# One written-out instruction order: a planner that knows the port shared by VectorE and GpSimd

## The chip, the cores and the metric

The kernel runs on one core of a Trainium2 chip. The metric is the device time of one execution in microseconds. A core has five engines with queues of their own: TensorE (PE, with its weight loads PEld), VectorE (DVE), ScalarE (ACT), GpSimd (POOL) and SyncE (SP), which issues the DMAs here. TensorE's clock has two levels, 1.2 and 2.4 GHz; the granted clock was full (1.00) in every stretch of the profile but the last microseconds.

## The reference

Attention over 4 batches, 8 heads, 768 positions and head size 64, in which a position sees itself, the 127 before it (`window` = 128) and the first four (`n_sink` = 4). Its output, as 3072 rows of 512, goes through a gated layer of 1536 units:

```
scores = q @ k.T / sqrt(64);  keep = (pos < n_sink) | (0 <= rel < window)
a = softmax(where(keep, scores, -1e9));  attn = a @ v
x = attn as [3072, 512]
out = (sigmoid(x @ w_gate) * (x @ w_val)) @ w_out
```

Inputs to the attention are float32, the three weight matrices float64. The output is float32.

## The kernel before

The kernel is one long straight program. The work is described to a planner (`Plan`), which simulates the engines on the host while the program is built, and writes all instructions out in the order that its simulation gave. The hardware then keeps that order on each engine. Every instruction recorded by the planner has line 575, so groups are told apart by tiles.

A step of work (`Plan.op`) has a priority (smaller is more urgent) and a list of ways, each with an engine and a time in ns. In `run`, each engine that is free takes its most urgent ready step for which buffers are free. The second and third way of a step wait at a priority that is worse by 1 and 2. The times come from small formulas: `vec`, `act`, `pool` and `mac`. Three more things set the order. All times on DVE, ACT and POOL are multiplied by `CROWD` = 1.1 until 350 us. Up to `HELD` = 45 us, an engine leaves a step aside when a more urgent one that only waits for steps under way becomes due within `HOLD` = 0.6 of the step's length. PE gets filler matmuls (`warm`, m<-ident) up to 130 us where too little of a period was busy.

The work itself:

- 96 attention units (`attend`, u = 0 to 95), one for each group of 256 positions and each head, with priority u. The first 20 are in plain float32. In the others each operand is split into a rounded high part and the rest (`copy` makes the high part, on ACT or else DVE; `rest` the difference, on POOL or else DVE). A unit does its scores on PE (tiles a), mask and row minimum on DVE, exp on ACT, the sum's reciprocal, a scaling of P, a transpose on PE, a split of the transposed P (wt) with two selections on POOL, the product with v on PE, and two additions on DVE (low, xf).
- 36 decodings of the float64 weights (`decode`, tiles wst to ws), each a load, a scaling on ACT, a byte step (ACT, or DVE, or POOL) and two integer steps on DVE. Their priorities are `DS1 + DR1 * n` = 8 + 0.3 n, on the attention units' scale. After the last of them (`DECODED`) the tiles lo may be loaded.
- The weights are then split too (`halves`, priority from 16 on; `thirds`, sums for the paired feed, from 250 us on, priority from 25 on); the low parts go to DRAM and come back as tiles lo, chunk by chunk.
- The feed (`feed`): nine chunks of rows, in plain float32 for the first, then single or double groups (`feed_plain`), and three chunks with two groups at once (`feed_pair`, seven products instead of eight). Each has 12 passes over f: products into m on PE, tanh on ACT, DVE steps into th and cv, a split into gh and gl, and the last products into o or a. Its steps on DVE and ACT come before all others (priority from -1000 on), on PE after the attention (10000 on).

Of the kernel before, what the change touches and what calls it, by code (L numbers as in the profile page):

```python
# [28 lines left out]
FLOOR = 0.75  # L29
CROWD = 1.1  # L30
HOLD = 0.6
HELD = 45000.0
GAP = 1.5
# [10 lines left out]
DS1 = 8.0  # L44
DR1 = 0.3
DS2 = 18.0
# [5 lines left out]
ALT = 1  # L52
# [240 lines left out]


class Op:
    def __init__(self, prio, ways, dma, busy):
# [5 lines left out]
class Plan:  # L302
# [37 lines left out]
    def run(self, warm, fill_ns, fill):  # L340
# [13 lines left out]
        def put(o):  # L354
            for i, (e, _, _) in enumerate(o.ways):
                heapq.heappush(waiting[e], ((o.prio + i * ALT, o.seq), o))

# [8 lines left out]
        dma_free, window, active, cold = 0.0, 1, [0.0] * 1000, True  # L366
        HAM = 4096 / 1.2

        def busy(a, b, frac):
# [6 lines left out]
        while events:  # L376
# [25 lines left out]
            for e in free:  # L402
# [4 lines left out]
                while waiting[e] or unsure:  # L407
# [25 lines left out]
                    if first != e and BACK:  # L433
# [5 lines left out]
                        if wait < BACK:  # L439
                            held.append((key, o))  # L440
                            continue
                    ns, fn = next((ns, fn) for w, ns, fn in o.ways if w == e)
                    if e in soon and now < HELD:
                        soon[e] = [x for x in soon[e] if x.due > now and id(x) not in done]
                        if any(
                            x.prio + GAP < o.prio and x.due < now + HOLD * ns for x in soon[e]
                        ):
                            held.append((key, o))
                            continue
# [4 lines left out]
                    if e in "VAG" and now < CROWDED:  # L454
                        ns *= CROWD
                    if e == "PE":
                        while window * HAM <= now:
                            x = active[window - 1] / HAM
                            cold = x < HOT if cold else x < WARMED
                            window += 1  # L460
                        if cold:
                            ns *= 2
                        busy(now, now + ns, o.busy)
# [44 lines left out]
def kernel(  # L508
# [71 lines left out]

    def vec(cols, fast=False):
        return 80 + (0.95 if fast else 1.25) * cols

# [3 lines left out]
    def pool(cols):  # L587
        return 250 + 2.2 * cols

# [5 lines left out]

    def copy(prio, cols, out, in_, r, w, psum=False, start=0.0):

        plan.op(
            prio,
            [  # L600
                ("A", act(cols, psum), lambda: A.copy(out=out(), in_=in_())),
                ("V", vec(cols, not psum), lambda: V.tensor_copy(out=out(), in_=in_())),
            ],
            r, w, start=start,
        )

    def rest(prio, cols, out, in0, in1, r, w, psum=False):

        plan.op(
            prio,  # L610
            [
                (
                    "G", pool(cols), lambda: G.tensor_tensor(
                        out=out(), in0=in0(), in1=in1().bitcast(F32), op=ALU.subtract
                    ),
                ),
                (
                    "V", vec(cols), lambda: V.tensor_tensor(
                        out=out(), in0=in0(), in1=in1().bitcast(F32), op=ALU.subtract
                    ),  # L620
                ),
            ][1 if psum else 0 :],
            r, w,
        )

    def f32(ap):
        return ap if ap.dtype == F32 else ap.bitcast(F32)
# [212 lines left out]
    def attend(u, b, h, t0, T, XR):  # L840
# [44 lines left out]
        for t in range(T):  # L885
# [28 lines left out]
            def exp(t=t):  # L914
# [6 lines left out]
            plan.op(  # L921
                u, [("V", 290 if first else 600, top)],
                [sc, (MASKS, 3), (MASKS, min(t0 + t, 2))], [sc, (P, t)],
# [21 lines left out]
        def mul():  # L945
            for t in range(T):
# [6 lines left out]
                )),  # L953
                ("G", 300, guard(G)), ("V", 300, guard(V)),
            ], [], [rs]
# [3 lines left out]
        )  # L959
        plan.op(u, [("G", 760, share), ("A", 720, mul), ("V", 720, scale)], [rs], [P])  # L960

        if not plain:
# [21 lines left out]
            plan.op(  # L984
                u, [("G", pool(W), spread(G)), ("V", vec(W), spread(V))], [turned, OWN], [sk]
            )
# [7 lines left out]
        def turn():  # L994
# [4 lines left out]
            if plain:  # L999
# [3 lines left out]
                )  # L1003

        def split():
            f = 1 - prev
            if T > f:
                G.affine_select(
                    out=w()[:, :, f:T, 0], in_=f32(w())[:, :, f:T, 1],
                    pattern=[[0, Z], [0, T - f], [-1, 128]], compare_op=ALU.is_gt, fill=0.0,  # L1010
                    base=0, channel_multiplier=1,
                )
            G.affine_select(
                out=w()[:, :, :, 1], in_=f32(w())[:, :, :, 1],
                pattern=[[0, Z], [0, T], [1, 128]], compare_op=ALU.is_ge, fill=0.0, base=0,
                channel_multiplier=-1,
            )
# [5 lines left out]
        if not plain:  # L1023
# [6 lines left out]
            )  # L1030
        plan.op(u, [("G", 980.0 if plain else 1370.0, split)], [], [wt])

        o = 64 * y
        if plain:
            vhl, sk = vraw, SK0[h // 2 % 2]
            copy(
                u, 128, lambda: sk()[o : o + T * NS], lambda: tp()[0 : T * NS, W : W + 128], [tp],
                [(sk, y)], True,
            )
        else:  # L1040
            vhl = tile([128, L, 2 * D], F32R, "vhl", BUFS["vhl"])
            copy(u, L * D, lambda: vhl()[:, :, 0:D], vraw, [vraw], [(vhl, 0)])
            rest(
                u, L * D, lambda: vhl()[:, :, D : 2 * D], vraw, lambda: vhl()[:, :, 0:D],
                [vraw, (vhl, 0)], [(vhl, 1)],
            )
# [118 lines left out]
    def minus(p, cols, out, a, b, r, w, add=False, start=0.0):  # L1165
        plan.op(
            p, [
                (
                    n, ns, lambda E=E: E.tensor_tensor(
                        out=out(), in0=a(), in1=b(), op=ALU.add if add else ALU.subtract  # L1170
                    ),
                ) for n, ns, E in (("G", pool(cols), G), ("V", vec(cols), V))
            ], r, w, start=start,
        )
# [26 lines left out]
    def decode(prio, src, whole):  # L1201
# [19 lines left out]
                )),  # L1221
                ("V", 900.0, lambda: V.tensor_scalar(
                    out=by(2), in0=by(1), scalar1=13, scalar2=None, op0=ALU.logical_shift_right
                )),
                ("G", 1300.0, lambda: G.tensor_scalar(
                    out=by(2), in0=by(1), scalar1=2.0**-13, scalar2=-8191.0 / 16384, op0=ALU.mult,
# [5 lines left out]
        plan.op(  # L1232
            prio, [("V", vec(512, True), lambda: V.tensor_scalar(
                out=ai(), in0=ai(), scalar1=3, scalar2=None, op0=ALU.logical_shift_left
# [3 lines left out]
        plan.op(  # L1238
            prio, [("V", vec(512), lambda: V.scalar_tensor_tensor(
                out=ai(), in0=hw(), scalar=-2147483641, in1=ai(), op0=ALU.bitwise_and,  # L1240
# [243 lines left out]
    def feed_pair(ci, tcs, f, O):  # L1484
# [22 lines left out]
        def turn(i, src, r):  # L1507
# [42 lines left out]
        plan.op(  # L1550
            pr, [("V", vec(512), lambda: V.scalar_tensor_tensor(
                out=th(), in0=th(), scalar=1.0, in1=cv(), op0=ALU.add, op1=ALU.mult
# [102 lines left out]
```

## Time and profile before

| | |
|---|---|
| median of 3 runs | 808.45 us (807.86 to 809.13) |
| profiled execution | 808.95 us, span 807.2 us |
| PE busy | 767.6 us, 95% |
| DVE busy | 636.8 us, 79% |
| POOL busy | 508.3 us, 63% |
| ACT busy | 440.6 us, 55% |
| DMA | 185.59 MB, mean 230 GB/s |

Busy time is the time in which an engine's instructions are recorded as running, waits for a port included. PE's ends are modelled, so that a very short gap between matmuls is not seen. A stretch's length less PE's busy time in it is PE's idle time there.

### The profile page before, as it was taken

The page shows a single profiled execution, that of the slowest core. Times are in us where ns is not written, and L with a number is a line of the kernel's source. Part 1 is how long each engine was busy: PE and PEld are TensorE (multiplying, and loading weights), DVE is VectorE, ACT ScalarE, POOL GpSimd, SP SyncE. Part 2 cuts the span into 40 slices and gives each one's busy share as a digit, 9 for nine tenths or more (in the row PEclk, how much of TensorE's full clock was granted, in tenths as well). Part 3 has the DMA queues.
Part 4 walks back from the last instruction along what each step waited for, and adds up shares of the span by engine and source line. Part 5 has one row for each costly group of instructions (what it writes and reads, how often), then busy time and mean ns, then how long its engine had stood idle before and what let it go on. Part 6 is the DMA issues. An engine that isn't in the chain of part 4 may idle for free. (4 is left out here: it accounts for less than half of the span.)

```text
span 807.2 us, 16573 instructions
## 1 busy us (share of the span) xinstructions
PE 767.6 (95%) x5084; PEld 686.2 (85%) x5084; DVE 636.8 (79%) x1806; ACT 440.6 (55%) x1258; POOL 508.3 (63%) x675
## 2 busy tenths in 40 slices
PE   7999988999999999999999998999999999999996
PEld 6876766799999888799889887899898899999995
DVE  5899889855999999968999999989999994444111
ACT  7788877624777655446776544467656651111200
POOL 4678788745688889646887776757777862111111
PEclk9999999999999999999999999999999999999998
DMA  6999985996777899886677666677776666666761
GB/s 157 231 272 283 302 249 180 340 293 204 223 235 240 258 335 307 289 272 203 203 239 238 217 204 193 201 249 248 223 223 204 188 218 187 208 193 215 226 188 57
DMA packets 137264, 185.59 MB, mean 230 GB/s; under 512 B 49360, under 2 KB 61648, under 8 KB 137168
## 3 DMA queue, kind: packets, MB, share of 16 engines
q1 hardware_dynamic: 137168, 184.45, 73.8%
q8 instruction: 43, 0.70, 0.3%
q14 instruction: 53, 0.43, 0.2%
HBM read 159.24 MB, written 25.17 MB: 228 GB/s over the span
## 5 line engine op out<-in xcount | busy, mean ns | idle before, releaser
L575 PE MATMUL m<-ws,ws 128*128 128x256 f32 x1680 | 316.1, 285 | 4.3 <-DVE th L575 2.9
L575 PE MATMUL m<-ws,lo 128*128 128x256 f32 x1272 | 293.1, 282 | 1.3 <-POOL ws L575 0.7
L575 PEld LDWEIGHTS m<-ws,ws 128*128 128x128 f32 x1680 | 265.6, 189 | 16.1 <-DVE th L575 4.2
L575 PEld LDWEIGHTS m<-ws,lo 128*128 128x128 f32 x1272 | 212.4, 189 | 2.2 <-DMA lo<-wlo_d 1.0
L575 POOL TENSOR_SCALAR_AFFINE_SELECT wt<-wt 128x512 fp32r<-128x512 f32 (+3 forms) x192 | 125.2, 652 | 41.0 <-DVE wt L575 20.7
L575 POOL TENSOR_TENSOR gl<-th,gh 128x256 fp32r<-128x256 f32 (+1 forms) x53 | 53.4, 1008 | 123.7 <-DVE gh L575 89.4
L575 ACT ACTIVATE th<-m 128x256 f32<-128x256 f32 x108 | 41.5, 384 | 127.7 <-PE m L575 78.9
L575 ACT ACTIVATE P<-P,negm_all 128x144 f32<-128x144 f32 x192 | 78.8, 411 | 38.1 <-DVE negm_all L575 36.1
L575 DVE SCALAR_TENSOR_TENSOR th<-th,m 128x256 f32<-128x256 f32 x72 | 29.8, 414 | 64.3 <-PE m L575 63.2
L575 PE MATMUL o<-ws,gh 128*128 128x512 f32 x192 | 77.2, 402 | 1.3 <-DVE total L1606 0.8
L575 PE MATMUL o<-ws,gl 128*128 128x512 f32 x192 | 75.9, 395 | 1.1 <-DVE gl L575 0.7
L575 PE MATMUL o<-lo,gh 128*128 128x512 f32 x192 | 75.1, 391 | 0.0
L575 DVE CUSTOM_DVE_ANT_0 P<-a,am 128x144 f32<-128x144 f32 x192 | 58.5, 305 | 10.2 <-PE a L575 4.0
L575 POOL TENSOR_TENSOR ws<-ws,ws 128x512 fp32r<-128x512 f32 (+1 forms) x47 | 60.7, 1298 | 6.9 <-ACT ws L575 2.6
L575 PE MATMUL a<-wt,vhl 128*128 128x256 f32 (+2 forms) x282 | 61.2, 327 | 3.2 <-POOL wt L575 2.3
L575 POOL TENSOR_TENSOR hi<-qkT,hi 64x256 fp32r<-64x256 f32 x60 | 49.9, 832 | 15.7 <-issue 5.6
L575 PEld LDWEIGHTS a<-wt,vhl 128*128 128x128 f32 x282 | 47.1, 189 | 13.3 <-POOL wt L575 4.8
L575 ACT CAST hi<-qkT 128x656 fp32r<-128x656 f32 (+1 forms) x70 | 49.2, 704 | 10.5 <-PE a L575 6.7
L575 PE MATMUL a<-ident,P 128*128 128x128 f32 (+1 forms) x212 | 40.4, 277 | 9.9 <-POOL P L575 3.3
L575 DVE TENSOR_TENSOR cv<-m,cv 128x256 f32<-128x256 f32 x72 | 30.0, 417 | 24.8 <-ACT cv L575 14.7
L575 PE MATMUL a<-hi 128*128 128x272 f32 (+1 forms) x152 | 44.8, 305 | 3.0 <-DVE negm_all L575 1.1
L575 POOL TENSOR_TENSOR kl<-qkT,hi 128x400 fp32r<-128x400 f32 (+1 forms) x43 | 45.3, 1053 | 1.6
(144 smaller groups left out, 1723.5 us busy)
## 6 DMA issues: line engine op xcount, KB each, us to landing
lo<-wlo_d SPq DMA_DIRECT2D x396, 256.0 KB, 3.4
wlo_d<-ws SPq DMA_DIRECT2D x72, 256.0 KB, 4.4
qkT<-in_qk_dram SPq DMA_DIRECT2D x52, 328.0 KB, 3.9
qkT<-in_qk_dram SPq DMA_DIRECT2D x24, 264.0 KB, 3.8
wst<-in_moe_w_gate_dram SPq DMA_DIRECT2D x12, 512.0 KB, 5.4
wst<-in_moe_w_val_dram SPq DMA_DIRECT2D x12, 512.0 KB, 5.2
wst<-in_moe_w_out_dram SPq DMA_DIRECT2D x12, 512.0 KB, 4.8
out_dram<-w SPq DMA_DIRECT2D x24, 256.0 KB, 3.7
```

Source lines behind the costliest of these rows:

```text
L575: return lambda *a, **kw: tc.keep_in_program_order(op(*a, **kw))
```

## The change

Some costs get a mark, `Port`: steps on DVE that read two SBUF operands or copy and scale within SBUF, and all large steps on POOL. The planner holds one time, `port`, up to which the port is taken. A marked step is lengthened by its wait for the port, less `LEAD` = 130 ns, and then takes the port. On DVE a marked step is left aside until the port is within 230 ns of free. A marked way of a step whose first way is ACT is left aside while ACT has under `BACKA` = 500 ns ahead of it. `CROWD` becomes 1.0 (no stretching), `HELD` 800 us (the holding rule is on throughout), `DR1` 0.2 (decodings at 8 + 0.2 n). The third way of a step now waits like the second. Costs are set anew, and the two selections on POOL are two steps of the plan. The core of the diff:

```diff
-CROWD = 1.1
+CROWD = 1.0
+LEAD = 130.0
+PWAIT = 100.0
+BACKA = 500.0
+ALTR = 1.0
-HELD = 45000.0
+HELD = 800000.0
-DR1 = 0.3
+DR1 = 0.2
+class Port(float):
+    pass
...
-                heapq.heappush(waiting[e], ((o.prio + i * ALT, o.seq), o))
+                alt = ALT if o.ways[0][0] == "A" else ALTR
+                heapq.heappush(waiting[e], ((o.prio + min(i, 1) * alt, o.seq), o))
...
+                    through = isinstance(ns, Port)
+                    if through and first == "A" and BACKA:
+                        mine = (o.prio, o.seq)
+                        wait = max(free[first] - now, 0.0) + sum(
+                            x.ways[0][1] for k, x in waiting[first]
+                            if k < mine and id(x) not in done and x.ways[0][0] == first
+                        )
+                        if wait < BACKA:
+                            held.append((key, o))
+                            continue
+                    if through and e == "V" and port - LEAD - PWAIT > now:
+                        held.append((key, o))
+                        n += 1
+                        heapq.heappush(events, (port - LEAD - PWAIT, n, None))
+                        continue
...
+                    if through:
+                        ns += max(0.0, port - now - LEAD)
+                        port = now + ns + (70.0 if e == "V" else 0.0)
...
-    def vec(cols, fast=False):
-        return 80 + (0.95 if fast else 1.25) * cols
+    def vec(cols):
+        return 80 + 1.0 * cols
+    def one(cols):
+        return Port(75 + 0.52 * cols)
+    def two(cols):
+        return Port(60 + 1.07 * cols)
     def pool(cols):
-        return 250 + 2.2 * cols
+        return Port(170 + 2.17 * cols)
...
-                ("V", vec(cols, not psum), lambda: V.tensor_copy(out=out(), in_=in_())),
+                ("V", vec(cols) if psum or apart else one(cols), lambda: V.tensor_copy(out=out(), in_=in_())),
...
-                ("V", 900.0, lambda: V.tensor_scalar(
+                ("V", Port(900.0), lambda: V.tensor_scalar(
-                ("G", 1300.0, lambda: G.tensor_scalar(
+                ("G", Port(1340.0), lambda: G.tensor_scalar(
...
-        plan.op(u, [("G", 980.0 if plain else 1370.0, split)], [], [wt])
+        plan.op(u, [("G", Port(180 + 0.9 * Z * (T - f) * 128), split)], [], [wt])
+        plan.op(u, [("G", Port(180 + 0.9 * Z * T * 128), rest_of)], [], [wt])
```

## Rows read from the trace of the kernel before

**Rows 1.** Page, part 1: busy us (share of the span) xinstructions.

```profile
PE 767.6 (95%) x5084; PEld 686.2 (85%) x5084; DVE 636.8 (79%) x1806; ACT 440.6 (55%) x1258; POOL 508.3 (63%) x675
```

**Rows 2.** Stretches: length, busy of PE, PEld, DVE, ACT, POOL, clock, DMA, GB/s.

```profile
40.00:120.00 80.00, 74.43 (x348) 55.58 (x347) 71.97 (x170) 63.73 (x139) 63.54 (x71) 1.00 0.90 277
...
120.00:160.00 40.00, 34.84 (x202) 27.80 (x201) 35.05 (x97) 29.77 (x72) 32.54 (x41) 1.00 0.79 257
...
160.00:280.00 120.00, 119.57 (x859) 112.35 (x859) 96.69 (x310) 69.59 (x222) 83.55 (x127) 1.00 0.79 243
...
280.00:340.00 60.00, 55.31 (x367) 48.56 (x366) 59.52 (x131) 32.48 (x93) 50.00 (x57) 1.00 0.93 310
...
380.00:520.00 140.00, 132.29 (x915) 120.71 (x914) 133.40 (x389) 84.57 (x261) 104.46 (x139) 1.00 0.69 214
...
520.00:660.00 140.00, 138.46 (x956) 126.17 (x956) 132.35 (x378) 86.71 (x262) 104.27 (x134) 1.00 0.72 221
...
660.00:800.00 140.00, 139.04 (x963) 129.11 (x962) 48.52 (x117) 21.98 (x61) 26.56 (x31) 1.00 0.61 189
```

**Rows 3.** Timeline: start, us, instruction; one step in two consecutive passes.

```profile
697.71 0.39 PE L575 MATMUL a<-ws,gh 128*128 128x512 f32 x1
...
705.50 0.39 PE L575 MATMUL a<-ws,gh 128*128 128x512 f32 x1
```

**Rows 4.** Waits of PE, 160 to 700 us: total, times, longest.

```profile
PE m L575 <- DVE th L575: 2.9, 6, 0.6
```

**Rows 5.** Forms on PE, 120 to 160 us: busy, mean ns, idle before.

```profile
L575 PE MATMUL m<-ident 128*128 128x128 f32 x18 | 3.1, 280 | 0.0
```

**Rows 6.** Timeline, 284 to 289 us: DVE and GpSimd.

```profile
284.00 0.41 DVE L575 TENSOR_TENSOR gl<-th,gh 128x256 fp32r<-128x256 f32 x1
...
284.33 0.41 DVE L575 TENSOR_TENSOR ws<-ws,ws 128x256 f32<-128x256 f32 x1
...
288.52 1.24 POOL L575 TENSOR_TENSOR kl<-qkT,hi 128x400 fp32r<-128x400 f32 x1
...
288.77 1.27 DVE L575 TENSOR_TENSOR gl<-th,gh 128x256 fp32r<-128x256 f32 x1
```

**Rows 7.** Forms on DVE, 280 to 340 us.

```profile
L575 DVE TENSOR_TENSOR ws<-ws,ws 128x256 f32<-128x256 f32 x18 | 12.4, 687 | 0.0
...
L575 DVE TENSOR_TENSOR ws<-ws,ws 128x512 fp32r<-128x512 f32 x12 | 11.0, 927 | 0.0
...
L575 DVE TENSOR_TENSOR gl<-th,gh 128x256 fp32r<-128x256 f32 x8 | 6.2, 776 | 0.0
...
L575 DVE SCALAR_TENSOR_TENSOR th<-th,m 128x256 f32<-128x256 f32 x11 | 4.5, 408 | 0.0
```

**Rows 8.** Forms on DVE, 680 to 760 us.

```profile
L575 DVE SCALAR_TENSOR_TENSOR th<-th,cv 128x512 f32<-128x512 f32 x9 | 6.2, 693 | 0.9
...
L575 DVE CAST gh<-th 128x512 fp32r<-128x512 f32 x9 | 3.8, 427 | 0.3
```

**Rows 9.** Forms on DVE, 400 to 520 us.

```profile
L575 DVE SCALAR_TENSOR_TENSOR th<-th,cv 128x512 f32<-128x512 f32 x11 | 9.7, 879 | 0.5 <-ACT th L575 0.2
...
L575 DVE CAST st<-P 128x32 fp32r<-128x32 f32 x8 | 5.1, 644 | 0.6 <-POOL P L575 0.3 <-ACT P L575 0.2
...
L575 DVE CAST gh<-th 128x512 fp32r<-128x512 f32 x6 | 5.1, 854 | 0.0
```

**Rows 10.** Forms on ACT, 400 to 520 us.

```profile
L575 ACT CAST gh<-th 128x512 fp32r<-128x512 f32 x5 | 3.1, 621 | 2.9 <-DVE rs L575 2.0 <-DVE th L575 0.9
...
L575 ACT CAST st<-P 128x32 fp32r<-128x32 f32 x10 | 2.1, 213 | 2.7 <-DVE P L575 1.3 <-POOL P L575 1.3
```

**Rows 11.** Tile wst: count, ns min/median/max, first and last start.

```profile
L575 ACT ACTIVATE wst<-wst x26: 1330/1357/1384, 22.0 to 136.6; 128x512 uint16<-128x512 uint16 x26
...
L575 POOL TENSOR_SCALAR wst<-wst x10: 1338/1474/1755, 14.8 to 128.8; 128x512 uint16<-128x512 uint16 x10
```

**Rows 12.** Tile lo, its loads: the same columns.

```profile
L575 SPq DMA_DIRECT2D lo<-wlo_d x396: 319/320/1433, 139.7 to 788.1; - x198
```

More of the change, by code (lines that the diff above doesn't have):

```diff
@@ L367, in run @@
         HAM = 4096 / 1.2
+        port = 0.0
         def busy(a, b, frac):
@@ L594, in dma, with copy @@
         return plan.op(prio, [("Q", ISSUE, fn)], r, w, dma=ns, start=start, behind=behind)
-    def copy(prio, cols, out, in_, r, w, psum=False, start=0.0):
+    def copy(prio, cols, out, in_, r, w, psum=False, start=0.0, apart=False):
         plan.op(
@@ L617, in rest @@
                 (
-                    "V", vec(cols), lambda: V.tensor_tensor(
+                    "V", vec(cols) if psum else two(cols), lambda: V.tensor_tensor(
                         out=out(), in0=in0(), in1=in1().bitcast(F32), op=ALU.subtract
@@ L921, in attend @@
             plan.op(
-                u, [("V", 290 if first else 600, top)],
+                u, [("V", 260 if first else 535, top)],
                 [sc, (MASKS, 3), (MASKS, min(t0 + t, 2))], [sc, (P, t)],
@@ L953, in attend @@
                 )),
-                ("G", 300, guard(G)), ("V", 300, guard(V)),
+                ("G", Port(213), guard(G)), ("V", Port(100), guard(V)),
             ], [], [rs]
@@ L959, in attend @@
         )
-        plan.op(u, [("G", 760, share), ("A", 720, mul), ("V", 720, scale)], [rs], [P])
+        plan.op(u, [("G", Port(660), share), ("A", 720, mul), ("V", Port(555), scale)], [rs], [P])
         if not plain:
@@ L984, in attend @@
             plan.op(
-                u, [("G", pool(W), spread(G)), ("V", vec(W), spread(V))], [turned, OWN], [sk]
+                u, [("G", Port(610), spread(G)), ("V", two(W), spread(V))], [turned, OWN], [sk]
             )
@@ L1003, in turn, with rest_of @@
                 )
+        f = 1 - prev
         def split():
[L1006 to L1012, printed above, removed]
+            G.affine_select(
+                out=w()[:, :, f:T, 0], in_=f32(w())[:, :, f:T, 1],
+                pattern=[[0, Z], [0, T - f], [-1, 128]], compare_op=ALU.is_gt, fill=0.0,
+                base=0, channel_multiplier=1,
+            )
+        def rest_of():
             G.affine_select(
@@ L1041, in attend @@
             vhl = tile([128, L, 2 * D], F32R, "vhl", BUFS["vhl"])
-            copy(u, L * D, lambda: vhl()[:, :, 0:D], vraw, [vraw], [(vhl, 0)])
+            copy(u, L * D, lambda: vhl()[:, :, 0:D], vraw, [vraw], [(vhl, 0)], apart=True)
             rest(
@@ L1171, in minus @@
                     ),
-                ) for n, ns, E in (("G", pool(cols), G), ("V", vec(cols), V))
+                ) for n, ns, E in (("G", pool(cols), G), ("V", two(cols), V))
             ], r, w, start=start,
@@ L1232, in decode @@
         plan.op(
-            prio, [("V", vec(512, True), lambda: V.tensor_scalar(
+            prio, [("V", one(512), lambda: V.tensor_scalar(
                 out=ai(), in0=ai(), scalar1=3, scalar2=None, op0=ALU.logical_shift_left
@@ L1238, in decode @@
         plan.op(
-            prio, [("V", vec(512), lambda: V.scalar_tensor_tensor(
+            prio, [("V", two(512), lambda: V.scalar_tensor_tensor(
                 out=ai(), in0=hw(), scalar=-2147483641, in1=ai(), op0=ALU.bitwise_and,
@@ L1550, in feed_pair @@
         plan.op(
-            pr, [("V", vec(512), lambda: V.scalar_tensor_tensor(
+            pr, [("V", two(512), lambda: V.scalar_tensor_tensor(
                 out=th(), in0=th(), scalar=1.0, in1=cv(), op0=ALU.add, op1=ALU.mult
```

## The prediction

> **What bounds the kernel now.** I read the busy line of the page first, then the table of stretches, then the forms of DVE and ACT inside the stretches where PE falls short. PE is the bound over the whole span: 767.6 of 807.2 us [rows 1]. The profiled execution took 808.95 us, 1.75 us more than its span and 0.5 us above the 808.45 us median of the runs shown; my sums are made against 808.95. By stretch [rows 2] there are three kinds. From 160 to 280 us and from 660 to 800 us PE is busy all but 0.4 and 1.0 us, while DVE is at 81% and 35%: there is nothing to win there. One pass of the paired feed takes 705.50 - 697.71 = 7.79 us there [rows 3], with no gap in which anything but PE decides. From 280 to 340, 380 to 520 and 520 to 660 us PE lacks 4.69, 7.71 and 1.54 us, together 13.9, and DVE is busy 99%, 95% and 95%. These gaps are short and many; the row with the most is PE waiting for DVE's result th on the feed's own path, 2.9 us in six times, 0.6 us at most [rows 4]. From 120 to 160 us PE lacks 5.16 us, and 3.1 us more went to 18 filler matmuls [rows 2, 5]. So at most about 22 us can be had (13.9 + 5.2 + 3.1), two thirds of it where DVE is full.
>
> **Why DVE is full.** Part of its busy time is waiting for GpSimd. One subtraction of 256 columns took 0.41 us alone and 1.27 us when it began 0.25 us into a 1.24 us GpSimd subtraction [rows 6]: it ended 0.28 us after GpSimd did, so it had the port 0.13 us of its own length early. Instructions with one operand in PSUM don't show it: 408 ns in the fullest stretch [rows 7]. From 280 to 340 us the excess is 18 x (687 - 410) + 12 x (927 - 693) + 8 x (776 - 410) ns = 10.7 of 60 us [rows 7, 8]. From 380 to 520 us the same forms that are undisturbed late (693 and 427 ns) take 879 and 854 [rows 8, 9].
>
> **The change, part by part.** No instruction's arithmetic changes and none is added; a few may be done by another engine, and the order on each engine is different.
>
> Costs. The old costs were averages with the collisions in them: 720 ns for a two-input step of 512 columns on DVE, 566 for a copy, times 1.1 up to 350 us. The new ones are 608 and 341. Alone, the rows have 693 and 427 [rows 8], and of such a duration about 0.08 us lies beside the next instruction: two steps of 0.41 us started 0.33 us apart [rows 6], where the new cost of 256 columns is 334 ns. So 693 and 427 stand for 613 and 347 from start to start, and a PSUM step of 256 columns, which goes from 400 to 336, for 408 - 80 = 328 [rows 7]. The new lone durations are right within 3%. By itself this moves no time; I cost it at nothing between -2 and +2 us (less than that largest sum of waits [rows 4], with either sign), since the order it gives is judged in the next steps.
>
> The port. DVE's port steps are now put off by the planner until the port is within 230 ns of free, and PSUM steps go in between. What that can give is bounded by how much port time there is. From 280 to 340 us GpSimd holds it 50.0 us [rows 2] and DVE's three largest groups need 26 x 0.41 + 12 x 0.69 = 18.9 us [rows 6, 7, 8], 69 us in 60, less 0.13 us at each of about 2 x 38 handovers, 10 us: 59 of 60. The port itself is full there, so sorting alone gives little. I take 1.5 of the 4.69 us: the share is that of what is done by DVE instead of GpSimd (0.41 us for 256 columns; GpSimd's 1.24 us for 400 [rows 6] make it about 0.8, an estimate); bounds 0 and 4.69. From 380 to 520 us GpSimd has 104.5 of 140 us, DVE's spare is 6.6 us, and a sorting that gives back half of the excess that I can see there, 11 x 186 + 6 x 427 = 4.6 us, gives 2.3 us.
>
> The Trainium skill, "SBUF — State Buffer", section "Who interferes with whom", says that the port pair is an exclusive lock, held for the whole instruction, and that the order of issue decides who blocks. The 1.27 us row agrees, except that the late one started 0.13 us before the other's recorded end. By that rule alone the sum of port time can't be lowered by sorting, which is the second rival below.
>
> Copies. A copy that has ACT as first choice is now taken by DVE (or GpSimd) through the port only when ACT has 500 ns or more ahead of it. In 400 to 520 us two such groups cost DVE 5.1 + 5.1 us, waiting included [rows 9]; on ACT the same fourteen take 8 x 213 + 6 x 621 ns = 5.4 us [rows 10], and ACT has 55 us idle of the 140 [rows 2]. If two thirds go, DVE gets 7 us back in a stretch where it has 6.6 spare, so its spare doubles. The cost is a later copy: 621 against 427 ns, 0.2 us on the feed's path for the six, 1.2 us, hidden wherever PE has another tile's work. I take 3.5 us from 380 to 660 us for port and copies together beyond the 2.3; bounds 0 and 9.25 less 2.3 = 6.95.
>
> The selection step on GpSimd becomes two entries in the plan instead of one. It is the same 192 instructions; another may now stand between the two. Nothing, within +-0.3 us.
>
> Closer decoding. The 36 decoding steps have the due times 8.0 to 15.0 instead of 8.0 to 18.5, so each is ahead of up to 3.5 attention units that stood ahead of it. The low halves are first loaded at 139.7 us, after the last decoding at 136.6 [rows 11, 12], and the next chunk's feed can't begin before. Decoding's byte step takes 1.36 us on ACT and 1.47 on GpSimd [rows 11]; the new rule for copies moves some of the ten on GpSimd to ACT, which is at 80% from 40 to 120 us [rows 2]: the nearest price is ten times 1.36 = 14 us of ACT, where it has 16.3 idle up to 120 us and 10.2 after. I expect the last decoding 5 us earlier. PE gains only what it lacked from 120 to 160 us, 5.2 + 3.1 = 8.3 us; I take 3.5, because some of that lack is attention waiting on its own chain [rows 2, 5]. Bounds -3 (ACT late, decoding no earlier) and 8.3. What is late next is PE itself, as from 160 us.
>
> Holding to the end. The rule that leaves an engine idle when something more urgent is due within 0.6 of the step's length was off after 45 us and is now on. Where DVE is 95% busy that is paid from its 6.6 us of spare [rows 2]; I cost it at nothing, hidden by the spare that the copies make. If that cover is gone it is the third rival.
>
> Sum: 1.5 + 2.3 + 3.5 + 3.5 = 10.8 us; 808.95 - 10.8 = 798.2, or 797.7 against the median. I predict **798 us**.
>
> **Rivals.** (1) All of it works: the 13.9 us from 280 to 660 and the 8.3 us go. 808.95 - 22.2 = 787 us. For it: DVE names most gaps. Against: the port is full at 280 to 340 us. (2) No change: the port's time is conserved, DVE's waits only become waits of GpSimd, and the earlier decoding finds PE with other work. 808.5 us. For it: the 59 of 60 above, and ACT's idle time shows that the copies were not the only limit. Against: 380 to 520 us, where port and PE both have room. (3) Slower: holding eats DVE. From 280 to 660 us, without the stretch 340 to 380, DVE runs 898 instructions [rows 2]; a hold lasts at most 0.6 x 0.41 = 0.25 us for the short ones, and 0.12 on average. If one in five is held, 180 x 0.12 = 22 us, against a spare of 0.5 + 6.6 + 7.7 = 14.8 us: 7 us late, and the gains from 280 us on (7.3) don't come, while the 3.5 us of decoding do: 808.95 + 7 - 3.5 = 812; at one in four, 27 us, 817. It decides from one in eight on (14.8 / 0.12 = 123 of 898). Against it: the held engine is released by steps that DVE itself ends, so many holds are zero.
>
> **How the numbers follow.** The forecast 0.53, with a range of its own of 793 to 804; all of it 0.14; no change 0.12; slower 0.21. Faster than before by over 0.2% (1.6 us, about what a measurement of this kernel can tell from no change) is 0.53 + 0.14 = 0.67; within it 0.12; slower 0.21. The range must leave out no more than 0.2: 785 takes in the first rival, 814 all of the second and half of the third.
>
> **What would show it.** Port: from 380 to 520 us, DVE's two-input step of 512 columns nearer 693 than 879 ns, and DVE below 130 of 140 us. Copies: the counts of ACT's casts up, of DVE's down by about a third or more, ACT above 90 us in that stretch. Decoding: the first load of a low half at 132 to 136 us and fewer than 18 fillers after 120 us. The last stretch should have the same 7.79 us pass and start earlier by the whole gain, at about 650 us. The prediction is wrong if PE's idle time from 280 to 660 us stays at 12 us or more, if ACT becomes what the decoding steps wait for, or if DVE shows idle time from 280 to 660 us while PE waits for DVE.

## The result: 783.24 us, and the profile after

The changed kernel takes 783.24 us (median of 4 runs, 781.31 to 785.19) where the kernel before took 808.49 in the same session: a ratio of 0.969 [0.966, 0.971], 25 us less. The forecast was 798 us with a range of 785 to 814: the direction was right, the forecast gain of 10.8 us is less than half of what came, and the time lies below the range. The profiled execution took 783.63 us with a span of 781.8. Its busy line answers to [rows 1]; the recorded line is 603 now.

```profile
PE 756.3 (97%) x5068; PEld 684.8 (88%) x5068; DVE 588.4 (75%) x1759; ACT 468.5 (60%) x1335; POOL 490.2 (63%) x637
```

PE's count fell by 16, the fillers (78 before, 62 after); the rest of its work is the same. DVE lost 48 us of busy time and ACT gained 28. The stretches, to be laid beside [rows 2] (length, busy of PE, PEld, DVE, ACT, POOL, clock, DMA, GB/s), with four longer ones at the end:

```profile
40.00:120.00 80.00, 75.62 (x356) 57.08 (x355) 70.99 (x185) 69.75 (x136) 49.23 (x59) 1.00 0.94 284
120.00:160.00 40.00, 38.73 (x244) 33.32 (x243) 38.80 (x104) 32.65 (x91) 32.44 (x37) 1.00 0.89 304
280.00:340.00 60.00, 59.72 (x427) 55.70 (x426) 49.96 (x135) 36.28 (x105) 50.18 (x65) 1.00 0.81 259
340.00:380.00 40.00, 38.91 (x275) 36.22 (x274) 37.70 (x98) 27.46 (x84) 33.37 (x38) 1.00 0.98 341
380.00:520.00 140.00, 137.43 (x967) 127.01 (x967) 124.45 (x385) 89.50 (x285) 105.25 (x139) 1.00 0.76 232
520.00:660.00 140.00, 139.33 (x979) 129.76 (x979) 110.77 (x335) 77.83 (x236) 91.86 (x113) 1.00 0.71 220
...
0.00:160.00 160.00, 148.59 (x803) 120.36 (x804) 135.80 (x406) 132.61 (x316) 102.16 (x136) 1.00 0.88 265
260.00:380.00 120.00, 117.17 (x830) 109.12 (x829) 106.51 (x287) 79.11 (x233) 99.38 (x123) 1.00 0.86 285
380.00:660.00 280.00, 276.76 (x1944) 256.77 (x1944) 235.22 (x719) 167.33 (x519) 197.10 (x251) 1.00 0.73 226
660.00:760.00 100.00, 100.00 (x695) 93.24 (x694) 25.90 (x56) 22.26 (x53) 16.70 (x17) 1.00 0.66 205
```

The same view of the kernel before, for the longer stretches and for one in which PE is never late:

```profile
0.00:160.00 160.00, 142.86 (x750) 112.23 (x751) 136.24 (x387) 123.30 (x294) 117.81 (x155) 1.00 0.84 251
...
260.00:380.00 120.00, 114.82 (x795) 104.18 (x793) 108.61 (x279) 65.28 (x197) 87.30 (x112) 1.00 0.87 279
380.00:660.00 280.00, 270.75 (x1869) 246.89 (x1868) 265.75 (x766) 171.28 (x523) 208.73 (x273) 1.00 0.70 218
660.00:760.00 100.00, 100.00 (x693) 93.14 (x692) 41.99 (x97) 18.40 (x51) 19.72 (x22) 1.00 0.66 209
```

The counts in brackets say more than the busy time. Where PE is never late it starts 693 matmuls in 100 us, late in the kernel, or 859 in 120 us [rows 2], with attention among them: 0.144 and 0.140 us each. Counted at 0.144, the changed kernel is ahead by 69 useful matmuls up to 160 us (803 - 62 against 750 - 78), 9.9 us; by 35 from 260 to 380 us, 5.0; and by 75 from 380 to 660 us, 10.8. From 160 to 260 us both have the same (715 and 716). Together 25.7 us, where the profiled executions differ by 25.3. Matmuls are of several lengths, so each share is an estimate; the sum (25.1 at 0.140) shows that it is a fair one. The last stretch runs at the rate of before, 695 in 100 us, so nothing was won there, as forecast.

### The profile page after: what moved, and what is told of

The parts are those of the page before. It is cut to its first block, busy times and chain, and to the rows that moved or that the text cites. A ratio compares the mean times of both kernels' runs of the same rounds, so it can differ in the third digit from the quotient of the medians.

```text
span 781.8 us, 16405 instructions
## 1 busy us (share of the span) xinstructions
PE 756.3 (97%) x5068; PEld 684.8 (88%) x5068; DVE 588.4 (75%) x1759; ACT 468.5 (60%) x1335; POOL 490.2 (63%) x637
## 4 chain that ended last, share of the span: by engine, by line
PE 68%; DVE 13%; DMA 7%; ACT 3%; issue 2%; POOL 1%; POOLq 0%; DVEq 0%; ACTq 0%
PE m L603 38%; PE a L603 15%; PE o L603 15%; DMA wst<-in_moe_w_val_dram 5%; DVE ws L603 3%; DVE th L603 2%; DVE P L603 1%; DVE vhl L603 1%; ACT ws L603 1%; ACT wst L603 1%; DVE kl L603 1%; DVE xf L603 1%; DVE wt L603 1%; DVE low L603 1%; DMA out_dram<-w 1%
## 5 line engine op out<-in xcount | busy, mean ns | idle before, releaser
L603 POOL TENSOR_TENSOR gl<-th,gh 128x256 fp32r<-128x256 f32 (+1 forms) x73 | 73.6, 1008 | 137.6 <-ACT gh L603 108.2
L603 ACT CAST gh<-th 128x256 fp32r<-128x256 f32 (+1 forms) x96 | 46.6, 486 | 81.0 <-DVE th L603 79.6
L603 POOL TENSOR_TENSOR sk<-turned,own 128x256 fp32r<-128x256 f32 x55 | 38.0, 691 | 14.9 <-DVE turned L603 11.0
L603 DVE COPY_PREDICATED a<-tri,a 128x128 f32<-128x128 int32 x160 | 45.5, 284 | 2.1 <-PE a L603 1.8
L603 PEld LDWEIGHTS o<-ws,gl 128*128 128x128 f32 x192 | 36.0, 187 | 10.8 <-DVE gl L603 1.6
L603 ACT ACTIVATE wst<-wst 128x512 uint16<-128x512 uint16 x33 | 44.8, 1359 | 0.7
```

Source lines behind the costliest of these rows:

```text
L603: return lambda *a, **kw: tc.keep_in_program_order(op(*a, **kw))
```

## The experiments

The theories, as the expectations name them. A: the parts of the change work as meant (decoding, port, copies). B: the holding rule matters, beside the port. C: any other order moves the time by some microseconds, whatever it is for. D: the port's account pays only together with the copies rule. E: C holds, and the change moves the whole family of orders down by some 10 us. In each run I read the time, PE's count in the stretches above, and the first load of a low half (tile lo). "PE count" means matmuls started.

### One part undone, or one part alone

**Closer decoding**, given to the kernel before (e1), and nearly taken from the changed one (e2):

```diff
-DR1 = 0.3
+DR1 = 0.2
```

> The kernel before with the decoding steps closer (0.2 instead of 0.3), nothing else. Theory A (decoding steps are worth the PE time that was lost from 120 to 160 us, about 8 us): 799 to 802 us, first load of a low half near 129 us as in the changed kernel. Theory B (the gain is the holding rule and the port, decoding finds PE with other work): 806 to 810 us. Theory C (any new order moves the time by some us either way, whatever the setting means): anywhere from 800 to 815.

```diff
-DR1 = 0.2
+DR1 = 0.28
```

> The changed kernel with decoding steps nearly as far apart as before (0.28). Theory A: 8 us minus a fifth is lost again, 789 to 791 us, with the first load of a low half at 136 us or later. Theory B: 782 to 785. Theory C: 783 to 795 with no relation to that load.

e1 took 806.01 us, ratio 0.996 [0.994, 0.998], and e2 791.88, 0.981 [0.978, 0.983]. **The holding rule** set back to 45 us (e3):

```diff
-HELD = 800000.0
+HELD = 45000.0
```

> The changed kernel with the holding rule off after 45 us, as before. Theory A (holding is paid from spare and is worth nothing): 782 to 786 us. Theory B (holding keeps DVE free for the feed's steps and is most of what PE got back from 280 to 660 us): 793 to 803. Theory C: 780 to 795.

e3 took 793.3 us, 0.981 [0.977, 0.984]. The first load of a low half tells the first two parts apart. Tile lo of the changed kernel (count, ns min/median/max, first and last start):

```profile
L603 SPq DMA_DIRECT2D lo<-wlo_d x396: 319/320/1752, 128.6 to 762.7; - x198
```

The same of e1, closer decoding alone:

```profile
L575 SPq DMA_DIRECT2D lo<-wlo_d x396: 319/320/2004, 140.2 to 787.4; - x198
```

Of e2, where decoding is nearly as wide as before:

```profile
L603 SPq DMA_DIRECT2D lo<-wlo_d x396: 319/326/1261, 128.2 to 768.4; - x198
```

And of e3, closer decoding without holding:

```profile
L603 SPq DMA_DIRECT2D lo<-wlo_d x396: 319/320/1447, 139.6 to 774.3; - x198
```

Closer decoding alone leaves it at 140.2 us (139.7 before, [rows 12]); without closer decoding, but with holding, it is at 128.2; with closer decoding and no holding at 139.6. So the holding rule, which I had costed at nothing, brings the decoding forward, and the closer due times don't. e3's 10 us over the changed kernel are mostly there: up to 160 us it starts 691 useful matmuls (775 less 84 fillers) against 741, 7 us. e2's 9 us are elsewhere: 738 there, but 692 from 160 to 260 us and 819 from 260 to 380, against 715 and 830, 5 us of them. e3's time lies where theory B put it, but not for B's reason: from 380 to 660 us, without holding, PE starts 1938 matmuls, against 1944 with it. How the rule brings decoding forward shows from 40 to 125 us in the splits of weights, which are less urgent than a decoding step. The forms on ACT of the changed kernel there (busy, mean ns, idle before):

```profile
L603 ACT ACTIVATE wst<-wst 128x512 uint16<-128x512 uint16 x29 | 39.4, 1360 | 0.6
...
L603 ACT CAST ws<-ws 128x512 fp32r<-128x512 f32 x3 | 2.0, 656 | 0.0
```

and of e3:

```profile
L603 ACT ACTIVATE wst<-wst 128x512 uint16<-128x512 uint16 x23 | 31.3, 1359 | 0.0
...
L603 ACT CAST ws<-ws 128x512 fp32r<-128x512 f32 x18 | 11.0, 620 | 0.0
```

With holding ACT does 3 split copies instead of 18 (DVE takes 16 instead of 7) and 29 byte steps instead of 23 in the same 85 us: the plan keeps ACT free for the step that is about to be due. In the runs below the same line divides all orders: with holding throughout the first load is at 124.8 to 132.8 us (11 kernels; a twelfth, e5, breaks down as a whole), without it at 136.0 to 141.2 (8). Up to 160 us PE starts 714 to 750 useful matmuls with it (mean 736) and 661 to 703 without (mean 687): 49 on average, some 7 us. The kernel before with holding alone was not run.

**The copies rule** switched off (e4):

```diff
-BACKA = 500.0
+BACKA = 0.0
```

> The changed kernel without the rule that leaves copies to ACT while ACT has under 500 ns ahead of it. Theory A (copies give DVE about 10 us back where it is full): 787 to 792 us and DVE casts back at the counts of before. Theory B: 782 to 786. Theory C: 780 to 795.

815.94 us, 1.009 [1.006, 1.012]: 33 us lost, far more than any expectation. But not where the rule was to work: from 380 to 660 us PE starts 1948 matmuls, 4 more than with the rule. The loss is between 330 and 370 us. e4's stretches there:

```profile
320.00:330.00 10.00, 9.75 (x72) 9.04 (x71) 9.55 (x31) 6.90 (x21) 8.11 (x12) 1.00 0.61 178
330.00:340.00 10.00, 3.48 (x20) 2.61 (x18) 9.90 (x26) 8.73 (x25) 8.42 (x11) 0.80 1.00 349
340.00:350.00 10.00, 1.03 (x3) 0.71 (x3) 9.44 (x17) 8.31 (x19) 9.36 (x8) 0.50 1.00 356
350.00:360.00 10.00, 4.34 (x16) 3.83 (x16) 9.28 (x14) 2.52 (x7) 9.60 (x9) 0.50 1.00 367
360.00:370.00 10.00, 8.83 (x44) 7.64 (x43) 9.73 (x29) 5.29 (x17) 5.97 (x9) 0.67 0.50 147
370.00:380.00 10.00, 8.22 (x57) 7.19 (x56) 9.80 (x26) 6.64 (x21) 7.34 (x8) 1.00 0.53 154
```

and what PE waits for there (total, times, longest):

```profile
PE a L603 <- DVE kl L603: 8.8, 1, 8.8
PE a L603 <- POOL wt L603: 8.1, 1, 8.1
```

Two single waits of 8 to 9 us. As I read it, the feed has run out of weights just before the paired chunks, attention steps are all that PE has left, and those stand behind the sums and splits of weights (ws) that DVE and POOL are doing all at once. In e6 and e9 below the feed itself waits for such a piece (ws), 8.9 and 13.6 us at once. I call it the hole at the hand-over. From 260 to 380 us e4 starts 624 matmuls and the changed kernel 830; 206 x 0.144 = 30 of the 33 us.

**The port's account** removed, with the new lone durations left in (e5; the planner's latency setting is 182 ns in this and the next two runs):

```diff
-                    if through and e == "V" and port - LEAD - PWAIT > now:
+                    if False:
...
-                    if through:
-                        ns += max(0.0, port - now - LEAD)
-                        port = now + ns + (70.0 if e == "V" else 0.0)
```

> The changed kernel whose planner keeps no account of the port (steps through it are neither put off nor lengthened; costs, copies rule, holding and decoding as changed; the planner's latency 182 instead of 180 ns). Theory A (the account of the port is what shortens DVE's waits where it is full): 795 to 806 us, and the two-input step th<-th,cv of 512 columns back near 880 ns from 380 to 660 us. Theory B (the holding rule does it): 782 to 787. Theory C (any new order moves the time by some us): 780 to 800 with no relation to that step's duration.

881.46 us, 1.089 [1.085, 1.093]. That is outside all three expectations. From 160 to 260 us PE starts 530 matmuls where the others have about 710. My reading, which no other run tests, is that lone durations without the account promise work that the engines can't deliver, and that the old padded averages had been carrying the collisions. Taken so, the two edits are one, and this run does not price the account. The next two were meant to: **the port's account with the new costs** (e9: no copies rule, old holding, old decoding; the split selections and the new waiting of third ways are still in it) and **all but the account** (e10: the old costs and the old stretching by 1.1 beside the rules for copies, holding, decoding and third ways and the split selections).

```diff
-BACKA = 500.0
+BACKA = 0.0
...
-HELD = 800000.0
+HELD = 45000.0
...
-DR1 = 0.2
+DR1 = 0.3
...
```

> The changed kernel with the holding rule off after 45 us, decoding at 0.3 and no rule for copies: of the change, the account of the port, the lone costs and the split selection alone (latency 182). Theory A (the account of the port keeps PE fed where DVE is full): from 380 to 660 us PE idle at most 4 us and over 1930 matmuls, 793 to 800 us if the hand-over to the paired feed (300 to 380 us) has no hole, up to 815 with one. Theory D (port account helps only with the rule for copies): 915 or fewer matmuls from 380 to 520 us.

```diff
-CROWD = 1.0
+CROWD = 1.1
...
-                    if through and e == "V" and port - LEAD - PWAIT > now:
+                    if False:
...
-                        ns += max(0.0, port - now - LEAD)
-                        port = now + ns + (70.0 if e == "V" else 0.0)
...
-        return Port(60 + 1.07 * cols)
+        return Port(80 + 1.25 * cols)
...
```

> The kernel before with the other parts: old average costs, CROWD 1.1, no account of the port, but copies rule, holding throughout, decoding at 0.2 and split selection (latency 182). Theory A: 380 to 660 us as before, PE idle 7 to 10 us, 798 to 806 us (decoding's and copies' share). Theory D: 785 to 795.

e9 took 818.44 us, 1.013 [1.010, 1.015], and e10 816.6, 1.010 [1.008, 1.013]. Both have the hole (658 and 671 matmuls from 260 to 380 us), so their times say nothing of the parts; their counts outside it might. From 380 to 660 us, e9:

```profile
380.00:660.00 280.00, 275.79 (x1927) 254.76 (x1926) 217.75 (x656) 143.12 (x442) 172.12 (x223) 1.00 0.71 219
```

and e10:

```profile
380.00:660.00 280.00, 272.31 (x1905) 251.00 (x1904) 250.89 (x727) 170.09 (x530) 205.43 (x262) 1.00 0.73 222
```

That is 58 and 36 more matmuls than before's 1869. But both runs have the latency setting 182, and the kernel before with nothing but that setting (e8, below) starts 1933 there:

```profile
380.00:660.00 280.00, 275.47 (x1933) 255.06 (x1932) 251.53 (x738) 161.29 (x489) 188.77 (x252) 1.00 0.72 220
```

So these two runs price neither part. Theory D named 915 or fewer matmuls from 380 to 520 us for e9; it starts 966, but e8 starts 959, so this tells nothing of the copies rule either.

### Settings that mean nothing

The hole came with edits that have nothing to do with it, so I moved two settings that describe nothing new to the planner: the latency between engines that it assumes (`LAT`, 180 ns) and the time from which the weight sums start (`THIRDS`, 250 us). First the latency, to 178 and 170 ns in the changed kernel and to 182 in the one before:

```diff
-LAT = 180.0
+LAT = 178.0
```

> The changed kernel with the planner's latency between engines at 178 instead of 180 ns: a setting that stands for no mechanism, to see how far an order moves by itself. Theories A and B: 781 to 786 us. Theory C: off by 5 us or more, either way.

```diff
-LAT = 180.0
+LAT = 170.0
```

> The same with 170 ns. Theories A and B: 780 to 787 us. Theory C: off by 5 us or more, either way, and not by as much as with 178.

```diff
-LAT = 180.0
+LAT = 182.0
```

> The kernel before with the planner's latency at 182 instead of 180 ns, nothing else. Theories A and B: 806 to 811 us. Theory C: off by 5 us or more, either way.

Two nanoseconds in the planner cost 29 us: e6 took 812.21 us, 1.004 [1.002, 1.006]. e7 took 794.78, 0.983 [0.980, 0.987]; e8 804.29, 0.995 [0.992, 0.997]. e6 has the hole:

```profile
330.00:340.00 10.00, 4.07 (x25) 3.19 (x23) 9.74 (x25) 7.70 (x21) 7.14 (x9) 0.86 1.00 337
340.00:350.00 10.00, 3.96 (x13) 3.19 (x13) 9.36 (x20) 8.98 (x22) 9.76 (x9) 0.50 1.03 376
350.00:360.00 10.00, 2.44 (x11) 2.45 (x12) 10.00 (x14) 3.70 (x11) 9.84 (x9) 0.50 0.91 343
```

If the hole is the cause, giving the sums of e6 more time must close it (e11). The same earlier start goes to the changed kernel (e12):

```diff
-THIRDS = 250000.0
+THIRDS = 230000.0
-LAT = 180.0
+LAT = 178.0
```

> The changed kernel with latency 178 (812.2 us), and the sums for the paired feed allowed from 230 instead of 250 us. Theory A (what separates the neighbours is one hole, PE out of feed while those sums are still to be made): the hole of 20 us at 320 to 360 us goes or shrinks below 8 us, 785 to 797 us. Theory C (any order is as likely as another): the hole stays, or another opens, 800 to 815.

```diff
-THIRDS = 250000.0
+THIRDS = 230000.0
```

> The changed kernel with those sums allowed from 230 us. Theory A: it has hardly a hole (4.6 us less PE time than full from 260 to 380 us), so 779 to 786 us. Theory C: off by 5 us or more, mostly slower.

e11 took 785.27 us, 0.972 [0.970, 0.975], and the hole is gone (829 matmuls from 260 to 380 us, 671 in e6):

```profile
330.00:340.00 10.00, 10.00 (x75) 9.49 (x74) 5.77 (x19) 5.02 (x17) 6.05 (x10) 1.00 0.97 318
340.00:350.00 10.00, 10.00 (x70) 9.17 (x69) 3.67 (x8) 3.15 (x9) 2.08 (x3) 1.00 0.72 207
```

The same edit opened a hole in the changed kernel: e12 took 802.95 us, 0.994 [0.992, 0.996], with 698 matmuls there, and 10 us of its span look like this:

```profile
320.00:330.00 10.00, 3.65 (x17) 2.45 (x15) 2.42 (x3) 5.67 (x12) 8.67 (x8) 0.78 0.97 324
```

So the hole is what separates such orders, and neither setting closes it by rule: each new order falls into it or not. It is not the same in all of them. In e4 and e6 DVE is full in it. In e12 DVE had waited 8.2 us for the store of a low part (DMA wlo_d<-ws) while GpSimd went through the sums; in e10 PE waits 16.2 us for ACT's copy of an output (w), and DVE is busy 0.42 of 10 us from 360 us on. The DMA engines are nearly full in the hole (0.91 to 1.05 in the rows above), but so they are in the changed kernel, without a hole:

```profile
340.00:350.00 10.00, 10.00 (x74) 9.44 (x73) 8.89 (x30) 8.60 (x27) 8.80 (x11) 1.00 1.03 379
```

Neither a full DVE nor full DMA engines make the hole by themselves, and no run changes the load of the DMA alone. Then the question is what the change does to all orders. The sums from 230 us for the kernel before (e13), from 270 for both (e14, e15), a latency of 188 ns for both (e16, e17), and the sums from 255 us for the changed one (e18); each differs from its parent in that one line:

```diff
-THIRDS = 250000.0
+THIRDS = 230000.0
```

> The kernel before with the sums for the paired feed allowed from 230 us: the partner of the changed kernel with 230 (803.0 us). Theory C (a setting that means little moves either kernel by some 10 us): 798 to 815 us. Theory E (C, and the change moves the whole family of orders down by about 10 us): slower than its partner by 5 to 20 us, 808 to 823.

```diff
-THIRDS = 250000.0
+THIRDS = 270000.0
```

> The kernel before with those sums allowed from 270 us. Theory C: 795 to 820 us. Theory E: 5 to 20 us slower than its partner below.

> The changed kernel with those sums allowed from 270 us. Theory C: 783 to 815 us, as likely above its partner as below. Theory E: 785 to 805, and below its partner. In both, the time follows PE's idle time from 260 to 380 us, which later sums should make longer: 5 to 20 us.

```diff
-LAT = 180.0
+LAT = 188.0
```

> The kernel before with the planner's latency at 188 ns. Theory C: 795 to 820 us. Theory E: 800 to 815, and slower than the changed kernel with 188.

> The changed kernel with the planner's latency at 188 ns, the partner of the kernel before with 188. Theory C: 783 to 815 us, above or below its partner. Theory E: 785 to 805, 5 to 20 us below its partner.

```diff
-THIRDS = 250000.0
+THIRDS = 255000.0
```

> The changed kernel with the sums for the paired feed allowed from 255 instead of 250 us, the smallest step of that setting. Theory C: 783 to 815 us, no nearer to 783 than the larger steps. Theory E with a smooth dependence: 781 to 788.

| setting | kernel before, us | changed kernel, us | difference |
|---|---|---|---|
| as written | 808.49 | 783.24 | -25.3 |
| latency 188 | 798.18, 0.988 [0.986, 0.991] (e16) | 791.37, 0.979 [0.977, 0.981] (e17) | -6.8 |
| sums from 230 | 811.59, 1.003 [1.001, 1.004] (e13) | 802.95 (e12) | -8.6 |
| sums from 270 | 804.12, 0.996 [0.994, 0.998] (e14) | 784.83, 0.971 [0.968, 0.974] (e15) | -19.3 |
| sums from 255 | | 784.51, 0.970 [0.969, 0.972] (e18) | |

The four pairs differ by -15.0 us on average, with a standard error of 4.4 (their spread, 8.8, over the root of 4); with so few pairs a 95% interval goes from 1 to 29 us. The three without the order as written give -11.6. With e6, e7, e11 and e18 the changed kernel's eight orders lie between 783.2 and 812.2 us, mean 792.4; with e8 the five of the kernel before between 798.2 and 811.6, mean 805.3. The means are 12.9 us apart. Theory E fits best: the change is worth some 12 to 15 us, with that uncertainty, and the order as written is the fastest of its eight. None of the others beats it; e18, e15 and e11 come within about 2 us. Two expectations failed in detail: e16 lies below the 800 us that E named, and later sums did not lengthen PE's idle time from 260 to 380 us in e15 (2.0 us, 2.8 in the changed kernel).

The counts split the gain. Up to 160 us the holding rule's 7 (above); from 160 to 260 us the eight orders start 9 fewer than the five, 1 us lost. From 380 to 660 us the twelve orders with the port's account start 1907 to 1956 matmuls, mean 1937; the seven with the old costs (e10 among them) 1869 to 1933, mean 1894: 43, some 6 us, with ranges that overlap (e8's 1933 lies among the twelve). e3 (1938) and e4 (1948) show that neither holding nor the copies rule is needed for it; the account, the new costs and the split selections are together in all twelve. From 260 to 380 us the means of the eight and the five are 788 and 778, 1.4 us, inside a spread of 671 to 830.

## Why the prediction was wrong

**The bound failed first**, and it is why the range ended at 785. "So at most about 22 us can be had" added up the time in which PE was recorded idle. Much of a late PE is not recorded so. In the changed kernel's timeline at full rate (start, us, instruction) a matmul of 256 columns is recorded for 0.28 us and the next one starts 0.12 us later:

```profile
354.74 0.28 PE L603 MATMUL m<-ws,lo 128*128 128x256 f32 x1
354.86 0.40 PE L603 MATMUL m<-ws,ws 128*128 128x256 f32 x2
355.10 0.28 PE L603 MATMUL m<-ws,lo 128*128 128x256 f32 x1
```

A start that is up to 0.16 us late leaves no gap. From 280 to 340 us before, 367 matmuls took 55.31 us of "busy" time [rows 2], 0.151 each; the 427 after took 59.72, 0.140. From 280 to 340 and 380 to 660 us the recorded idle time fell from 13.9 to 3.5 us, by 10.4, while PE started 135 more matmuls, 19.4 us' worth. A better bound was in the same trace: from 160 to 280 us, with feed and attention mixed and PE not late, it started 716 matmuls per 100 us [rows 2]. At that rate the 400 us from 260 to 660 hold 2864; 2664 (795 + 1869) were started. The 200 missing are 28 us at 0.14 each, before anything is won up to 160 us; the recorded idle time had said 14. The weight loads, PEld, say the same: 112.35 of 120 us, 93.6%, at full rate [rows 2], and 104.18 + 246.89 = 351.1 of the 400, which full rate would have done in 375: 25 us to be had. After the change they are 365.9, 9 us short, so 16 were won, as the counts say (5.0 + 10.8). The Trainium skill, "Perfetto Trace Analysis", section "Identifying the Most-Contended Engine", warns that the busy share of matmuls is no measure of what is left on TensorE and asks for the share of the peak rate and the busy share of the weight loads instead; this trace agrees (93.6% at full rate, 351.1 of 400 us where PE was late), and I had not read it so.

**Closer decoding, 3.5 us, and holding, nothing**, are the step that failed in its mechanism. The gain up to 160 us is there and larger (about 10 us in this pair, 7 between the families); it comes from the holding rule (e1 to e3). I had priced holding only where DVE is full, after 280 us, and not where urgent decoding steps meet long splits. The third rival, that holding eats DVE, has its place and price from me (it would decide from one in seven on, not eight: 123 of 898) and didn't happen: in e3 PE starts 1938 matmuls from 380 to 660 us without holding, 1944 with it. Signs: the first load was expected at 132 to 136 us and is at 128.6; fillers after 120 us are gone (18 before, [rows 5]); the byte steps moved to ACT, as the rows that answer to [rows 11] show, and ACT was not the limit: DVE's decoding steps waited for them 1.4 us in all from 40 to 125 us. The rows:

```profile
L603 ACT ACTIVATE wst<-wst x33: 1337/1357/1379, 20.0 to 126.0; 128x512 uint16<-128x512 uint16 x33
...
L603 POOL TENSOR_SCALAR wst<-wst x3: 1330/1337/1405, 17.1 to 35.6; 128x512 uint16<-128x512 uint16 x3
```

**Port and copies from 380 us on, 2.3 + 3.5 = 5.8 us**: this pair shows 10.8, the families 6. The size fits the families, as far as their overlap allows, and is short for this order. The sign that I named for it was a poor one. Forms on DVE from 380 to 660 us, before:

```profile
L575 DVE SCALAR_TENSOR_TENSOR th<-th,cv 128x512 f32<-128x512 f32 x25 | 22.3, 891 | 0.8 <-ACT th L575 0.2
L575 DVE TENSOR_TENSOR sk<-turned,own 128x256 fp32r<-128x256 f32 x19 | 16.2, 853 | 0.1
...
L575 DVE CAST st<-P 128x32 fp32r<-128x32 f32 x17 | 8.4, 496 | 0.7 <-POOL P L575 0.3 <-ACT P L575 0.2
...
L575 DVE TENSOR_TENSOR st<-P,st 128x32 fp32r<-128x32 f32 x16 | 7.1, 443 | 0.1
L575 DVE CAST gh<-th 128x512 fp32r<-128x512 f32 x9 | 6.8, 757 | 0.1
```

and after:

```profile
L603 DVE SCALAR_TENSOR_TENSOR th<-th,cv 128x512 f32<-128x512 f32 x28 | 24.6, 880 | 1.6 <-ACT low L603 0.5
...
L603 DVE TENSOR_TENSOR st<-P,st 128x32 fp32r<-128x32 f32 x20 | 6.2, 312 | 0.1
...
L603 DVE TENSOR_TENSOR sk<-turned,own 128x256 fp32r<-128x256 f32 x8 | 5.1, 633 | 0.0
...
L603 DVE CAST st<-P 128x32 fp32r<-128x32 f32 x3 | 0.5, 174 | 0.6 <-POOL P L603 0.6
```

The two-input step of 512 columns still takes 880 ns in the mean (911 from 400 to 520 us, against 879 in [rows 9]), not "nearer 693". That mean hides a wide spread: the median is 730 ns after and 819 before, the longest 1807 and 1403; and in e9 the mean is 705. The other port steps are the ones that wait less: sk 633 instead of 853 ns, st 312 instead of 443.

To put a number on all of them I took each form's mean less the smallest mean that any run has for it, times its count. By that estimate DVE's steps from 380 to 660 us hold 48 us of waiting before and 24 after; 20 to 30 in the twelve orders with the port's account and 35 to 48 in the seven with the old costs. At the latency setting 182 it is 20 with the account (e9) and 35 without (e8, e10). GpSimd's waiting does not grow in exchange: 16 us before and 10 after. Fewer of these steps go through DVE after the change, so part of the fall may be that. The second rival (the port's time is conserved, DVE's waits become GpSimd's) falls all the same. Less waiting did not by itself give PE more: e8 and e9 start 1933 and 1927 matmuls. The Trainium skill, "SBUF — State Buffer", section "Who interferes with whom", calls the shared port pair an exclusive lock; the single collision of [rows 6], 1.27 us instead of 0.41, agrees. How much waiting there is in all is up to the order.

Copies did what I expected of them: all of gh's 512-column copies moved to ACT, and ACT was at 89.5 of 140 us from 380 to 520 us, DVE at 124.5 (forecast: about 90, and below 130). e4 shows that this was not needed for PE. Of my signs of being wrong, PE's idle time from 280 to 660 us did not stay (4.6 us). DVE did stand idle, 44.8 of 280 us from 380 us on, while PE waited for it only 1.5 us in all: that sign was badly chosen too.

**Port at 280 to 340 us, 1.5 us**: PE started 427 instead of 367 matmuls there, but 12 fewer from 340 to 380; 5 us net over the hand-over. My argument, 59 of 60 us of port time, was about a stretch whose work could be stretched: the weight sums, which kept DVE full up to 340 us before (the last began at 336), now go on (the last began at 354), and the feed runs meanwhile. It missed what decides here, whether PE runs dry while they are done, worth up to 30 us either way (e4, e6, e11). The first rival's 787 us is nearest to what came, but its reason, that all recorded idle time goes, is not the one.

**What stays open**: what the port's account, the copies rule, the split selections and the new costs are worth by themselves, and what makes the hole. Each one's removal makes a new order, and a new order alone moves the time by up to 29 us; it would take as many settings for each as for the whole. The same holds for 10 to 12 of the 25 us of this pair: they are the order's, and why this one fell well at the hand-over and after is not shown.

## What to carry to other kernels

A change to a planner's rules makes a new order everywhere, so time it over a few settings that mean nothing, in both kernels, before the difference is put down to the rule; here the single pair said 25 us and four pairs 15, from 7 to 25. Take what an engine can still gain from the instructions that it starts in a stretch against those in a stretch at full rate of the same trace, or for TensorE from the busy share of its weight loads, not from its recorded idle time. A rule that keeps engines free for urgent steps is to be priced where urgent steps stand behind long ones, not where the engine is busiest.

## What the runs showed of the hardware

A hole costs more than its waits, since the clock falls. In e4 PE was busy 1.03 of 10 us from 340 us, and the granted clock was 0.50 (1.2 GHz) there and in the next 10 us, 0.67 in the next and 1.00 only from 370 us on. From 320 to 380 us it was idle 24.3 us and started 206 matmuls where 60 us at 0.144 hold 417, a loss of 30 us; starts that are late without a gap may be part of the difference. In e4's timeline the matmuls of 256 columns start 0.21 us apart at that clock, those of the changed kernel above 0.12:

```profile
354.69 0.41 PE L603 MATMUL a<-wt,vhl 128*128 128x256 f32 x1
354.90 0.41 PE L603 MATMUL a<-sk,vshl 128*128 128x256 f32 x1
355.11 0.63 PE L603 MATMUL a<-ident,P 128*128 128x128 f32 x2
```
